# Exponentials folded in place behind the first product with v, one-step splits of q and k, a new planned order, and 23 early weight quarters

## The chip, the cores and the metric

The kernel runs on one core of one Trainium2 chip. The metric is the device time of one execution in microseconds; the time of a kernel is the median of its runs. A difference of less than about 0.5% can't be told from none here: the three runs shown below already lie within 0.4% of each other.

## The reference

Causal attention with a forget gate for 8 batches of 8 heads (576 positions, head size 64), and then a soft mixture of 8 experts over all 8 x 576 = 4608 tokens of width 512. All arrays are float32.

```python
scores = scale * np.matmul(q, k.transpose(0, 1, 3, 2))           # scale = 1/8
cum = np.cumsum(np.maximum(s, 0.0), axis=-1)
bias = -(cum[:, :, :, None] - cum[:, :, None, :])
scores = np.where(causal, -1000000000.0, scores + np.minimum(bias, 0.0))
scores = scores - np.max(scores, axis=-1, keepdims=True)
attn = np.exp(scores)
attn = attn / (np.sum(attn, axis=-1, keepdims=True) + 1e-09)
attn_out = np.matmul(attn, v)
...
x = attn_out.transpose(0, 2, 1, 3).reshape(B * S, H * D)
logits = x @ phi                                # 4608 x 32 slots
d = softmax(logits, over tokens);  slot_input = d.T @ x
h = relu(slot_input[e] @ w1[e]);  slot_out[e] = h @ w2[e]        # 4 slots for each expert
c = softmax(logits, over slots);  out = c @ slot_out
```

phi is 512 x 32, w1 is 8 x 512 x 1024, w2 is 8 x 1024 x 512: 33.6 MB of weights.

## The kernel before

**The work.** The heads are taken two at a time: 32 pairs, four for each batch, head 0 of a pair on partitions 0 to 63 and head 1 on 64 to 127. The scores proper are held with the keys on the partitions and the queries along the row, in five key blocks of 128, 128, 128, 128 and 64; what is zero by causality is left out but for the diagonal, so that one head's exponentials are rows of 576 + 448 + 320 + 192 + 64 = 1600. For a pair p the steps are:

- `load` (L268): q and k arrive by one DMA, 128 x 1152. `cast` (L278, ACT) rounds them to the reduced float type in which PE multiplies, `low` (L283, DVE) subtracts to get the remainder; both in two steps of 576, q and then k. `cum` (L293) brings the gate's sums into the tile g by DMA, `md` (L359) the row maxima.
- `mx` (L311, PE): a first set of scores, of the rounded parts alone and with the queries on the partitions, in groups `mx.0` to `mx.3`, for the row maxima; `red` (L323, DVE) takes the maxima. `f0` (L338 and L339, POOL) splits them in two parts, `f1` (L346, PE) transposes them, `f2` (ACT) copies, `md` sends them into g.
- `s` (L377, PE): the scores proper, three products of the parts and one with g, in four groups `s.0` to `s.3`. `ex` (L388, ACT) writes the exponentials into the pair's p buffer, `cut` (L395, POOL) zeroes what lies above the diagonal.
- The fold: the five key blocks are added up to one row of 576 in a z buffer of its own. `zc` (ACT) copies the first 128 columns, and `z.0` to `z.3` (L421, L423, L425, L427, POOL; DVE for the last pair) add the blocks.
- `ax` and `a` (L467 and L478, PE) are the first product with v in the text's words: the exponentials times v. ACT copies it out (`evx`, `ev`) into a u buffer.
- `sm` (L507, PE), the closing sum: 16 small products of z with `onesl`, a table of 16 blocks of ones, add up over the partitions. The four pairs of a batch collect in one bank. After a batch's last pair DVE takes reciprocals, a DMA writes them out (`rs<-sr`) and one for each pair reads them back spread over partitions (`rd`, L517, `arena<-rs`); `nr` (L540, DVE) multiplies. In the last batch pairs 28 and 29, pair 30, and pair 31 close apart.
- For each batch then: transposes (`nat`, L548), logits (`lt`, L619 and L623), softmax over slots (`s0` to `s2`; its last product, `s2p`, is L682 on POOL, `e_nat`), and the softmax over tokens as a running sum (`t2` to `t8`: L733, L756, L771), which gives slot inputs.

After the 32 pairs: slot inputs (`sit`, L941), the two products with the experts' weights (`mlp1`, L954; `mlp2`, L988), and the outputs (`po`, L1020; L1028), 18 transfers of 0.524 MB.

**The order.** Every step is declared with `op(key, engine, planned ns, due time, function, what it waits for, banks)`. Due times are two for each pair plus a number from the table `PR`. `schedule()` (L34) lists the steps in order by planned starts, with six PSUM banks for scores, maxima and transposes; the engines get exactly that order, so on each engine nothing overtakes. Where the plan shows PE idle before the first product with v, and after the last one, 128x128 dummy products (`busy`, L914) are inserted, one for each 300 ns.

**Buffers.** `NBUF` counts them in one tile, the arena: two p, one z, and so on. A p buffer is free for the pair after next when the product with v and the fold have read it.

**The weights.** They come in 64 quarters of 0.524 MB. The first `NPRE` = 21 go to a place of their own (`pre`) one for each pair from pair 4 on, without waiting for anything but a load of q and k; the others follow (`get`, L836), on the same SP queue, into g, w and arena chunks as these come free near the end, and then into the places of used weights (`refill`).

The initial memory fills stand ahead of everything else on DVE and POOL, with the sum of the gates on DVE.

Of the kernel before, what the change touches and what calls it, by code (L numbers as in the profile page):

```python
# [20 lines left out]
PR = dict(load=-9.063, load_v=-9.132, cast=(9.576, 4.001), cum=-25.895, low=(4.9, 44.265), mx=(-6.08, 10.156, 8.807,  # L21
          8.159), red=(2.144, 3.397, 3.057, -37.226), f0=-0.714, f1=30.964, f2=0.529, md=-6.393, s=(-65.95, -10.099,
          -16.585, -0.002), ex=(6.942, -14.568, 1.896, 3.855), cut=(1.377, -17.534, 2.864, 12.095), zc=3.583,
          z=(1.07, -54.955, 7.483, 3.74), ax=102.687, a=(136.656, 0.022, -2.121, 0.386, -0.338), evx=-22.47,
          ev=-3.276, sm=14.037, e1=-1.61, rw=24.679, rd=-39.652, nstep=4.53, nr=1.749, nat=48.432, natd=-28.53,
          lt=-51.395, nat0=116.745, natd0=17.779, c0=4.561, c1=-16.819, soft=15.188, tok=30.263, LA=161.4, ct=1.864,
          T2=-19.79, LP=176.8, gap=0.81401)
# [75 lines left out]
def tile_attn_softmoe(ctx: ExitStack, tc, qk, v, s, phi, w1, w2, cst, out):  # L103
# [74 lines left out]
    nc.vector.tensor_scalar(s_sb, s_sb, 0.0, 8.0, op0=ALU.max, op1=ALU.mult)  # L178
    nc.vector.tensor_tensor_scan(out=cum, data0=ones_s, data1=s_sb, initial=0.0,
                                 op0=ALU.mult, op1=ALU.add)  # L180
    cumhl = reg("x", 0)[0:NH, 0:2 * S].rearrange("p (l x) -> p l x", l=2)
    nc.vector.tensor_copy(cumhl[:, 0, :].bitcast(F32R), cum)
    nc.vector.tensor_tensor(cumhl[:, 1, :].bitcast(F32R), cum, cumhl[:, 0, :], op=ALU.subtract)
    cumd = pd.tile([NH, 2, S], F32, tag="cum", name="cumd", bufs=1)
# [10 lines left out]
    nc.gpsimd.memset(reg("x", 0)[64:128, 0:DM], 0.0)  # L195
    for i in range(NV):
        nc.gpsimd.memset(reg("v", i)[64:128, 512:640], 0.0)
    for i in range(NPB):
        nc.gpsimd.memset(reg("p", i).rearrange("p (a x) -> p a x", a=2)[64:128, :, 1536:1600], 0.0)
    ph = one.tile([128, HP, 4 * NS], F32, name="ph")  # L200

    QO, KO = PAD, PAD + S
    gs = []
    for i in range(NG):
        t = slot("g", [128, PAD + 2 * S], F32R, f"g{i}")
        if i == 1:

            mask = one.tile([128, S], F32, name="mask")  # L210
            nc.gpsimd.memset(mask, 0.0)
            nc.gpsimd.affine_select(mask[:, S - 128:S], mask[:, S - 128:S], pattern=[[-1, 128]], compare_op=ALU.is_ge,
                                    fill=NEG, base=0, channel_multiplier=1)
        (nc.vector if i else nc.gpsimd).memset(t.bitcast(F32), 0.0)
        for a in (0, 64):
            nc.gpsimd.memset(t[a:a + 4, 0:KO].bitcast(F32), 1.0)
            nc.gpsimd.memset(t[a:a + 4, KO:].bitcast(F32), -1.0)  # L217
        gs.append(t)
    ws = []
    for i in range(NW):  # L220
        t = slot("w", [128, PAD + 4 * S], F32R, f"w{i}")
        nc.gpsimd.memset(t[:, 0:PAD].bitcast(F32), 0.0)
        ws.append(t)
# [30 lines left out]
    def scores(p):  # L254

        t0 = 2.0 * p
        gt, w = gs[p % NG], ws[p % NW]
# [17 lines left out]
        def cast(i):
            use("raw", p, NR)
            own("w", p, NW)
            nc.scalar.copy(w[:, QO + S * i:QO + S * (i + 1)], st["raw", p][:, i, :])  # L278

        def low(i):  # L280
            use("raw", p, NR)
            use("w", p, NW)
            nc.vector.tensor_tensor(w[:, QO + S * (2 + i):QO + S * (3 + i)], st["raw", p][:, i, :],  # L283
                                    w[:, QO + S * i:QO + S * (i + 1)].bitcast(F32), op=ALU.subtract)
# [828 lines left out]
```

## Time and profile before

| | |
|---|---|
| time, median of three runs (all of them) | 446.05 us (446.85, 446.05, 444.98) |
| profiled execution, and its span | 441.82 us, 440.1 us |
| mean granted PE clock | 0.978 of full speed |
| busy: PE, DVE, POOL, ACT | 406.3, 309.6, 281.4, 245.4 us (92%, 70%, 64%, 56%) |
| main DMA queue | 82.29 MB, 59.6% of 16 engines' time |
| HBM read, written | 71.84 MB, 10.06 MB |

The profile is of one execution, 1% faster than the median of the others. PE is the tensor engine, DVE the vector engine, ACT the scalar engine, POOL a second, general vector engine, and SP the engine that issues the DMAs; PE's weight loads overlap its products. In rows, "out<-in" are the program's names of the tiles, L478 is a line of the kernel, x20 a count of instructions. A row of the chain of work that ended last begins with start and duration in us. A timeline's row begins in the same way; what stands in brackets at its end is the idle time just before the row and what ended it. A row of a windows view has, after the window, its length, then busy time of PE, PE's weight loads, DVE, ACT and POOL (with the counts of instructions), the granted clock, the DMA share, and GB/s. In the row of clocks each digit is a fortieth of the span, in tenths of full speed.

### The profile page before, as it was taken

How to read it: one execution, taken by the hardware profiler on the slowest of the kernel's cores; microseconds unless marked ns; L12 is line 12 of the kernel's file. 1: busy time of each engine (PE TensorE's matmuls, PEld its weight loads, DVE VectorE, ACT ScalarE, POOL GpSimd, SP SyncE). 2: the span in 40 equal slices, each digit the busy share in tenths (PEclk: the TensorE clock that was granted, in tenths of full speed). 3: DMA queues.
4: the chain of work that ended last, by engine and by line, in shares of the span. 5: the costliest groups of instructions: out<-in, count | busy, mean ns of one | idle time of the engine just before them, and what ended most of it. 6: DMA issues, size and time to landing. Idle time of an engine off the chain costs nothing.

```text
span 440.1 us, 14686 instructions
## 1 busy us (share of the span) xinstructions
PE 406.3 (92%) x5625; PEld 302.5 (69%) x5625; DVE 309.6 (70%) x1055; ACT 245.4 (56%) x732; POOL 281.4 (64%) x385
## 2 busy tenths in 40 slices
PE   7999999989999999999999999999999999898960
PEld 6787777777677767766877687777776857344550
DVE  6777767987887888779877887788778486121460
ACT  3146676576658665856675676567665745011350
POOL 7349889878877895888588858887887710000000
PEclk9599999999999999999999999999999999999995
DMA  5317565626664475448544822362247389999988
GB/s 175 108 57 236 157 174 155 212 87 189 193 180 131 137 217 157 131 136 225 152 132 136 231 90 84 105 178 82 87 114 216 95 291 337 392 402 409 384 297 293
DMA packets 54549, 83.21 MB, mean 189 GB/s; under 512 B 5456, under 2 KB 41808, under 8 KB 54480
## 3 DMA queue, kind: packets, MB, share of 16 engines
q1 hardware_dynamic: 54480, 82.29, 59.6%
q8 instruction: 44, 0.72, 0.7%
q14 instruction: 25, 0.20, 0.1%
HBM read 71.84 MB, written 10.06 MB: 186 GB/s over the span
## 4 chain that ended last, share of the span: by engine, by line
PE 66%; DMA 12%; DVE 9%; issue 5%; SPq 3%; POOL 2%; ACT 1%; DVEq 0%
PE s L377 19%; PE y L478 15%; PE mx L311 10%; DMA arena<-rs 7%; PE m L954 3%; DMA rs<-sr 3%; PE m L988 3%; PE sum L507 3%; SPq L517 2%; DVE nmin L733 2%; PE busy L914 2%; PE lt L619 2%; PE nat L548 2%; PE po L1020 2%; DVE junk L323 1%
## 5 line engine op out<-in xcount | busy, mean ns | idle before, releaser
L323 DVE CUSTOM_DVE_ANT_0 junk<-mx,mask 128x448 bf16<-128x448 f32 (+3 forms) x320 | 125.5, 427 | 50.8 <-PE mx L311 25.1
L388 ACT ACTIVATE arena<-s 128x288 f32<-128x288 f32 (+4 forms) x384 | 114.3, 409 | 30.0 <-PE s L377 29.3
L377 PE MATMUL s<-w 64*128 64x288 f32 (+4 forms) x1152 | 109.2, 304 | 0.0
L478 PE MATMUL y<-arena 128*64 128x512 f32 (+4 forms) x640 | 90.1, 427 | 0.0
L377 PEld LDWEIGHTS s<-w 64*128 64x128 f32 (+1 forms) x1152 | 81.7, 177 | 10.1 <-ACT arena L388 1.2
L395 POOL TENSOR_SCALAR_AFFINE_SELECT arena<-arena 128x256 f32<-128x256 f32 (+1 forms) x160 | 69.0, 444 | 23.7 <-ACT arena L388 21.7
L478 PEld LDWEIGHTS y<-arena 128*64 128x64 f32 x640 | 43.0, 137 | 46.4 <-issue 35.8
L421 POOL TENSOR_TENSOR arena<-arena 128x896 f32<-128x896 f32 x31 | 66.4, 2141 | 7.5 <-PE mt L346 5.2
L311 PE MATMUL mx<-w 64*128 64x288 f32 (+4 forms) x384 | 59.3, 314 | 3.7 <-DVE e_nat L664 2.7
L311 PE MATMUL mx<-g,ones 64*128 64x288 f32 (+4 forms) x384 | 56.0, 308 | 1.7 <-DVE ones L227 1.7
L377 PE MATMUL s<-g 64*128 64x288 f32 (+4 forms) x384 | 56.5, 291 | 0.0
L423 POOL TENSOR_TENSOR arena<-arena 128x640 f32<-128x640 f32 x31 | 48.0, 1547 | 2.6
L278 ACT CAST w<-arena 128x576 fp32r<-128x576 f32 x64 | 39.8, 675 | 15.0 <-DMA arena<-in_qk_dram 15.0
L283 DVE TENSOR_TENSOR w<-arena,w 128x576 fp32r<-128x576 f32 x64 | 48.0, 776 | 0.0
L311 PEld LDWEIGHTS mx<-w 64*128 64x128 f32 x384 | 41.1, 190 | 8.1 <-PE s L377 3.8
L490 ACT COPY arena<-y 128x512 f32<-128x512 f32 x32 | 18.8, 588 | 47.0 <-PE y L478 47.0
L311 PEld LDWEIGHTS mx<-g,ones 64*128 64x128 f32 x384 | 41.0, 191 | 2.4 <-POOL g L217 1.9
L540 DVE TENSOR_TENSOR arena<-arena 128x576 f32<-128x576 f32 x31 | 34.7, 1128 | 8.7 <-DMA arena<-rs 8.4
L377 PEld LDWEIGHTS s<-g 64*128 64x128 f32 (+1 forms) x384 | 35.1, 177 | 0.7 <-DMA g<-hl 0.2
L338 POOL TENSOR_SCALAR mh<-mx 128x10 fp32r<-128x10 f32 x32 | 21.5, 672 | 20.4 <-DVE mx L323 20.3
L425 POOL TENSOR_TENSOR arena<-arena 128x384 f32<-128x384 f32 x31 | 31.4, 1013 | 2.4
L323 DVE CUSTOM_DVE_ANT_0 junk<-mx,mask,mx 128x288 bf16<-128x288 f32 x64 | 30.6, 516 | 2.2 <-PE mx L311 1.2
(157 smaller groups left out, 565.8 us busy)
## 6 DMA issues: line engine op xcount, KB each, us to landing
pre<-in_w_dram SPq DMA_DIRECT2D x38, 512.0 KB
arena<-in_qk_dram SPq DMA_DIRECT2D x32, 576.0 KB
...
```

The costliest lines, as they stand in the source:

```text
L278: nc.scalar.copy(w[:, QO + S * i:QO + S * (i + 1)], st["raw", p][:, i, :])
L283: nc.vector.tensor_tensor(w[:, QO + S * (2 + i):QO + S * (3 + i)], st["raw", p][:, i, :], w[:, QO + S * i:QO + S * (i + 1)].bitcast(F32), ...
L311: nc.tensor.matmul(ps[a][:, d:d + hi - lo], l[r], t[r, KO + lo:KO + hi], start=t is w, stop=t is gt)
L323: nc.vector.tensor_tensor_reduce(out=junk[r, 0:w], in0=ps[r, d:d + w], in1=mask[r, o:o + w], scale=1.0, scalar=m[:, a, 4:5] if i == 1 else ...
L377: nc.tensor.matmul(ps[a][0:n, d:d + hi - lo], t[r, ko + 128 * j:ko + 128 * j + n], t[r, qo + lo:qo + hi], start=x == 0, stop=x == 3)
L388: nc.scalar.activation(st["p", p][0:n, a, o + lo:o + hi], ps[0:n, d:d + hi - lo], AF.Exp, bias=0.0, scale=0.125)
L395: nc.gpsimd.affine_select(d, d, pattern=[[0, 2], [1, n]], compare_op=ALU.is_ge, fill=0.0, base=0, channel_multiplier=-1)
L421: eng.tensor_tensor(z[:, :, 128:576], pt[:, :, 128:576], pt[:, :, 576:1024], op=ALU.add)
L423: eng.tensor_tensor(z[:, :, 256:576], z[:, :, 256:576], pt[:, :, 1024:1344], op=ALU.add)
L425: eng.tensor_tensor(z[:, :, 384:576], z[:, :, 384:576], pt[:, :, 1344:1536], op=ALU.add)
L478: nc.tensor.matmul(y[r, lo - 64:512], vt[:, j, r], st["p", p][:, g, OFF[j] + lo - 128 * j:OFF[j] + 576 - 128 * j], start=(j == 0), stop=(j ...
L540: nc.vector.tensor_tensor(u, u, st.pop(("r", p)), op=ALU.mult)
```

## The change

It edits the program at these places:

1. The z buffer and `zc` are gone. The fold adds the blocks into the p buffer itself, at the columns where block 0 stands. Since the product reads these columns as exponentials, `z.0` waits for `a.0`, the product's first part (L469 in the new text). The closing sum reads the p buffer, and the exponentials of the pair after next wait for the sum.
2. `cast` and `low` are one step each of 1152 columns. Planned 1045 and 1500 ns instead of twice 565 and 950.
3. `onesl` is one row of 63 with a single column of ones, of which a window of 32 is taken; `phi` is stored once and not four times; `junk` and `en` have one buffer each, so that a batch's `sp` waits for the `ct` of the batch before.
4. The initial fills: `ones2` and `mx` come first on DVE, the mask and the first g tile first on POOL; the other two g tiles are steps of their own (`gi`) on POOL. The due times of pair 0's steps up to the exponentials are lowered by 200 (`tu`).
5. `NPRE` is 23. Without the z buffer the arena has 16 chunks for weights, not 17; With the places in g and w there were 22 quarters fetched by `get`, now 21, and 20 `refill` quarters follow instead of 21.
6. The table `PR` has other numbers throughout, which gives another order on every engine.

```diff
-NBUF = (2, 2, 2, 1, 5, 2, 3)
+NBUF = (2, 2, 2, 5, 2, 3)
-NPRE = 21
+NPRE = 23
...
-        for i in range(2):
-            op(("cast", p, i), "ACT", 565, (t0, ("cast", i)), (cast, i), [("load", p)] + war)
-            op(("low", p, i), "DVE", 950, (t0, ("low", i)), (low, i), [("cast", p, i)])
+        op(("cast", p), "ACT", 1045, (tu, "cast"), cast, [("load", p)] + war)
+        op(("low", p), "DVE", 1500, (t0, "low"), low, [("cast", p)])
...
-        war = [("a", g, j) for j in range(5)] + [("ax", g), ("z", g, 3), ("zc", g)] if g is not None else []
+        war = [("a", g, j) for j in range(5)] + [("ax", g), ("sm", g)] if g is not None else []
...
-            st["z", p] = reg("z", p % NZ).rearrange("p (a x) -> p a x", a=2)
-            nc.scalar.copy(st["z", p][:, :, 0:128], st["p", p][:, :, 0:128])
...
-            if i == 0:
-                eng.tensor_tensor(z[:, :, 128:576], pt[:, :, 128:576], pt[:, :, 576:1024], op=ALU.add)
-            elif i == 1:
-                eng.tensor_tensor(z[:, :, 256:576], z[:, :, 256:576], pt[:, :, 1024:1344], op=ALU.add)
...
+            n = 64 if i == 3 else 128
+            d = pt[0:n, :, 128 * (i + 1):576]
+            eng.tensor_tensor(d, d, pt[0:n, :, OFF[i + 1]:OFF[i + 1] + 448 - 128 * i], op=ALU.add)
...
-               zd[i] + [("z", p, i - 1) if i else ("zc", p)])
+               zd[i] + [("z", p, i - 1) if i else ("a", p, 0)])
...
-                        nc.tensor.matmul(y[o:o + 32, 0:SQ], onesl[:, 4 * hp + i, :], st["z", p][:, g, c:c + SQ],
+                        nc.tensor.matmul(y[o:o + 32, 0:SQ], onesl[:, 31 - 4 * hp - i:63 - 4 * hp - i], st["p", p][:, g, c:c + SQ],
...
-    for e, ns in (("DVE", 5200), ("POOL", 4200), ("SP", 1100), ("ACT", 2900), ("PE", 1100)):
+    for e, ns in (("DVE", 7000), ("POOL", 6200), ("SP", 700), ("ACT", 2900), ("PE", 1100)):
         op(("set", e), e, ns, (-1000,), lambda: None)
+    for i in range(1, NG):
+        op(("gi", i), "POOL", 2400, (2.0 * i - 10,), (ginit, i), [("set", "POOL")])
```

In the rows below, taken from the order of the instructions on an engine, there is no time; the number behind a tile's name is the pair or the batch with the group, and the last one counts tiles.

**The start, on SP's queue**, before: s is the gate, qk one pair's q and k, g the tile of gate sums and row maxima.

```order
L176 DMA arena_77<-in_s_dram 64x576
L447 DMA arena_77<-in_v_dram 128x4x128
L450 DMA arena_77<-in_v_dram 64x128
L268 DMA arena_77<-in_qk_dram 128x1152
L447 DMA arena_77<-in_v_dram 128x4x128
L450 DMA arena_77<-in_v_dram 64x128
L268 DMA arena_77<-in_qk_dram 128x1152
L293 DMA g0_128<-arena_77 2x1x576 x2
L293 DMA g1_134<-arena_77 2x1x576 x2
L293 DMA g2_145<-arena_77 2x1x576 x2
L268 DMA arena_77<-in_qk_dram 128x1152
L853 DMA cumd_101<-arena_77 64x1152
```

and now (L272 is the load of q and k, L296 the gate sums):

```order
L176 DMA arena_77<-in_s_dram 64x576
L272 DMA arena_77<-in_qk_dram 128x1152 x2
L438 DMA arena_77<-in_v_dram 128x4x128
L441 DMA arena_77<-in_v_dram 64x128
L438 DMA arena_77<-in_v_dram 128x4x128
L441 DMA arena_77<-in_v_dram 64x128
L296 DMA g0_123<-arena_77 2x1x576 x2
L296 DMA g1_124<-arena_77 2x1x576 x2
L272 DMA arena_77<-in_qk_dram 128x1152
L296 DMA g2_125<-arena_77 2x1x576 x2
L272 DMA arena_77<-in_qk_dram 128x1152
L846 DMA cumd_116<-arena_77 64x1152
```

The first two pairs' q and k stand ahead of all of v. On PE, 31 dummies stand ahead of the first maxima instead of 25, and all four groups of maxima of pair 0 ahead of the first of pair 1, where the group `mx.1` of pair 0 used to stand behind a group of pair 1; ahead of the first scores stand a transpose and four dummies, where eleven stood.

**A batch's third pair, on POOL**, batch 3 with pair 14, before (a fold is the rows L421, L423, L425, L427):

```order
L395 AFFINE_SELECT arena_77<-arena_77 128x2x128 x3
L395 AFFINE_SELECT arena_77<-arena_77 64x2x64
L421 TENSOR_TENSOR arena_77<-arena_77 128x2x448
L682 TENSOR_TENSOR e_nat_66<-e_nat_66,cs2_3373 128x160
L395 AFFINE_SELECT arena_77<-arena_77 128x2x128
L423 TENSOR_TENSOR arena_77<-arena_77 128x2x320
L425 TENSOR_TENSOR arena_77<-arena_77 128x2x192
L427 TENSOR_TENSOR arena_77<-arena_77 64x2x64
L338 TENSOR_SCALAR mh16_3481<-mx1_163 128x2x5
L339 TENSOR_TENSOR mh16_3481<-mx1_163,mh16_3481 128x2x5
```

and now (L398 cuts, L420 is the whole fold, L341 and L342 split the row maxima, L673 is the last product of the softmax over slots):

```order
L398 AFFINE_SELECT arena_77<-arena_77 128x2x128 x3
L398 AFFINE_SELECT arena_77<-arena_77 64x2x64
L398 AFFINE_SELECT arena_77<-arena_77 128x2x128
L341 TENSOR_SCALAR mh16_3364<-mx1_108 128x2x5
L342 TENSOR_TENSOR mh16_3364<-mx1_108,mh16_3364 128x2x5
L673 TENSOR_TENSOR e_nat_66<-e_nat_66,cs2_3417 128x160
L420 TENSOR_TENSOR arena_77<-arena_77 128x2x448
L420 TENSOR_TENSOR arena_77<-arena_77 128x2x320
L420 TENSOR_TENSOR arena_77<-arena_77 128x2x192
L420 TENSOR_TENSOR arena_77<-arena_77 64x2x64
```

The cuts stand ahead of the fold as a block, and the softmax's product, which stood behind the fold's first addition, stands ahead of it, as do the two steps on the maxima of pair 16.

**A plain pair, on PE**, the closing sum of pair 16 before:

```order
L311 MATMUL mx0_19_1_3918<-g1_134,ones2_157 128x288
L507 MATMUL sum16_3924<-arena_77,onesl_102 32x72 x16
L346 MATMUL mt_3950<-ident_61,mh18_3876 20x128
L548 MATMUL nat12_3952<-ident_61,arena_77 128x128 x4
L377 MATMUL s17_3_0_3964<-w2_155 128x320
```

and now:

```order
L314 MATMUL mx3_19_1_3875<-g1_124,ones2_102 128x192
L349 MATMUL mt_3891<-ident_61,mh18_3833 20x128
L498 MATMUL sum16_3897<-arena_77,onesl_97 32x72 x16
L314 MATMUL mx2_19_0_3927<-w1_132 128x448
L314 MATMUL mx2_19_1_3928<-w1_132 128x448
```

Before, the first product of pair 16 with v begins 32 rows behind this sum. Now it began 67 rows ahead of it, and the row of L469 that begins pair 17's stands 13 rows behind.

**The end, on PE**, before (L709 and L756 are transposes of the two softmaxes' rows, x and y the first product):

```order
L377 MATMUL s31_3_1_6890<-g1_134 128x320
L507 MATMUL sum30_6902<-arena_77,onesl_102 32x72 x16
L709 MATMUL ctb0_6926<-ident_61,en0_1861 96x128
L709 MATMUL cta0_6925<-ident_61,en0_1861 96x128 x4
L756 MATMUL dn6_6939<-ident_61,dt6_6811 128x128
L757 MATMUL dn6_6939<-ident_61,dt6_6811 64x128
L467 MATMUL x31_6943<-arena_77 64x64 x2
L478 MATMUL y30_6951<-arena_77 64x512 x2
```

and now:

```order
L380 MATMUL s31_3_1_6785<-g1_124 128x320
L498 MATMUL sum30_6802<-arena_77,onesl_97 32x72 x16
L700 MATMUL ctb0_6826<-ident_61,en0_1761 96x128
L700 MATMUL cta0_6825<-ident_61,en0_1761 96x128 x4
L747 MATMUL dn6_6839<-ident_61,dt6_6704 128x128
L748 MATMUL dn6_6839<-ident_61,dt6_6704 64x128
L469 MATMUL y31_6847<-arena_77 64x512 x2
```

Sum 30 used to stand ahead of product 30; now that product stands 53 rows ahead of it, with all of pair 31's scores between, and product 31 follows behind.

More of the change, by code (lines that the diff above doesn't have):

```diff
@@ L19 @@
 NG = 3
[L21 to L27, printed above, removed]
-NBUF = (2, 2, 2, 1, 5, 2, 3)
+PR = dict(load=-7.139, load_v=-2.32, cast=3.046, cum=-6.431, low=83.254, mx=(-43.805, 4.895, 4.715, 3.882),
+          red=(30.0, 18.855, 7.742, 5.31), f0=0.185, f1=23.061, f2=3.709, md=-16.796, s=(-21.112, -1.186, -26.288,
+          2.204), ex=(8.386, -2.546, 24.758, 5.631), cut=(13.379, 1.043, 13.216, -8.496), z=(5.742, 0.566, 8.913,
+          -16.511), ax=6.788, a=(2.526, -8.101, -13.574, -16.298, 7.51), evx=0.756, ev=-10.922, sm=14.574,
+          e1=-15.72, rw=-1.196, rd=-3.926, nstep=7.841, nr=0.118, nat=-32.994, natd=-18.393, lt=6.769, nat0=-3.935,
+          natd0=1.004, c0=-30.944, c1=-6.683, soft=25.805, tok=86.831, LA=142.6, ct=45.552, T2=45.669, LP=237.6,
+          gap=2.995)
+NBUF = (2, 2, 2, 5, 2, 3)
 NBANK = 6
 GAP = 300
-NPRE = 21
+NPRE = 23
 def schedule(ops, banks):
@@ L177, in tile_attn_softmoe @@
     nc.vector.memset(ones_s, 1.0)
[L178 to L184, printed above, removed]
     SQ = S // 8
-    onesl = one.tile([128, 4 * HP, 32], F32, name="onesl")
+    onesl = one.tile([128, 63], F32, name="onesl")
     nc.vector.memset(onesl, 0.0)
-    for a in range(4 * HP):
-        nc.vector.memset(onesl[:, a, a:a + 1], 1.0)
+    nc.vector.memset(onesl[:, 31:32], 1.0)
     dn = one.tile([128, 2, 128], F32, name="dn")
     nc.vector.memset(dn[64:128, 1, :], 0.0)
[L195 to L223, printed above, removed]
     ones2 = one.tile([128, 128], F32R, name="ones2")
@@ L232, in tile_attn_softmoe, with ginit @@
         mx.append(t)
+    nc.vector.tensor_scalar(s_sb, s_sb, 0.0, 8.0, op0=ALU.max, op1=ALU.mult)
+    nc.vector.tensor_tensor_scan(out=cum, data0=ones_s, data1=s_sb, initial=0.0,
+                                 op0=ALU.mult, op1=ALU.add)
+    cumhl = reg("x", 0)[0:NH, 0:2 * S].rearrange("p (l x) -> p l x", l=2)
+    nc.vector.tensor_copy(cumhl[:, 0, :].bitcast(F32R), cum)
+    nc.vector.tensor_tensor(cumhl[:, 1, :].bitcast(F32R), cum, cumhl[:, 0, :], op=ALU.subtract)
+    cumd = pd.tile([NH, 2, S], F32, tag="cum", name="cumd", bufs=1)
+    ph = one.tile([128, HP, NS], F32, name="ph")
+    mask = one.tile([128, S], F32, name="mask")
+    nc.gpsimd.memset(mask, 0.0)
+    nc.gpsimd.affine_select(mask[:, S - 128:S], mask[:, S - 128:S], pattern=[[-1, 128]], compare_op=ALU.is_ge,
+                            fill=NEG, base=0, channel_multiplier=1)
+    QO, KO = PAD, PAD + S
+    gs = [slot("g", [128, PAD + 2 * S], F32R, f"g{i}") for i in range(NG)]
+    def ginit(i):
+        t = gs[i]
+        nc.gpsimd.memset(t[:, 0:KO].bitcast(F32), 1.0)
+        nc.gpsimd.memset(t[:, KO:].bitcast(F32), 0.0)
+        for a in (0, 64):
+            nc.gpsimd.memset(t[a:a + 4, KO:].bitcast(F32), -1.0)
+    ginit(0)
+    ws = []
+    for i in range(NW):
+        t = slot("w", [128, PAD + 4 * S], F32R, f"w{i}")
+        nc.gpsimd.memset(t[:, 0:PAD].bitcast(F32), 0.0)
+        ws.append(t)
+    nc.gpsimd.memset(reg("x", 0)[64:128, 0:DM], 0.0)
+    for i in range(NV):
+        nc.gpsimd.memset(reg("v", i)[64:128, 512:640], 0.0)
+    for i in range(NPB):
+        nc.gpsimd.memset(reg("p", i).rearrange("p (a x) -> p a x", a=2)[64:128, :, 1536:1600], 0.0)
     OFF = [0, 576, 1024, 1344, 1536]
@@ L340, in f0 @@
             st["mh", p] = mh
-        op(("f0", p), "POOL", 850, (t0, "f0"), f0, [("red", p, i, a) for i in range(4) for a in range(2)] + [dep("f1", old(2))])
+        op(("f0", p), "POOL", 850, (tu, "f0"), f0, [("red", p, i, a) for i in range(4) for a in range(2)] + [dep("f1", old(2))])
         def f1():
@@ L347, in f1 @@
             st["mt", p] = ps
[L348 removed]
+        op(("f1", p), "PE", 110, (tu, "f1"), f1, [("f0", p), dep("md", old(2))], bank=1, ldw=17)
         def f2():
@@ L353, in f2 @@
             st["hl", p] = hl
-        op(("f2", p), "ACT", 160, (t0, "f2"), f2, [("f1", p)], frees=[(("f1", p), 0)])
+        op(("f2", p), "ACT", 160, (tu, "f2"), f2, [("f1", p)], frees=[(("f1", p), 0)])
         def md():
```

69 lines of the change are left out of this document (30 added, 39 removed).

## The prediction

> Times are microseconds. "Pair p" is a pair of heads, Y(p) the start of its first product with v on PE, and "fold" the four POOL additions that add up a pair's exponentials.
>
> **What bounds the kernel now.** I read the page's first rows, then the chain that ended last in order of time, then POOL's and DVE's instructions at the places that the change moves, then the tail by windows.
>
> ```profile
> span 440.1 us, 14686 instructions
> PE 406.3 (92%) x5625; PEld 302.5 (69%) x5625; DVE 309.6 (70%) x1055; ACT 245.4 (56%) x732; POOL 281.4 (64%) x385
> ...
> PEclk9599999999999999999999999999999999999995
> ...
> 43.96 2.81 PE s L377 x40
> ...
> 47.03 0.64 PE sum L507 x32
> ...
> 47.88 0.79 PE s L377 x8
> 48.67 1.41 PE mx L311 x20
> 50.08 2.74 PE y L478 x20
> 52.82 0.12 PE x L467 x4
> ```
>
> Up to about 375 PE sets the pace: a plain pair is these pieces and, where a line is left out, 0.26 of maxima and 0.21 of a transpose, without a gap: 8.96 from 43.96 to 52.94. POOL is nearly as full inside a pair:
>
> ```profile
> 184.43 2.12 POOL L421 TENSOR_TENSOR arena<-arena 128x896 f32<-128x896 f32 x1
> 186.50 0.41 POOL L395 TENSOR_SCALAR_AFFINE_SELECT arena<-arena 128x256 f32<-128x256 f32 x1
> ...
> 190.10 0.75 POOL L338 TENSOR_SCALAR mh<-mx 128x10 fp32r<-128x10 f32 x1
> 190.94 0.54 POOL L339 TENSOR_TENSOR mh<-mx,mh 128x10 fp32r<-128x10 f32 x1
> ```
>
> From the first row to the end of the last lie a fold's four additions and the two steps on the row maxima: 7.05, or 6.6 without the cut (L395 and its gap, 0.49) that stands among them; the two steps are 1.4 of it. The pair's other cuts, four of 0.41 or less, fill most of what is left of 8.96. The tail has other limits:
>
> ```profile
> 352.45 0.68 PE sum L507 x32
> ...
> 354.05 6.96 DMA rs<-sr
> ...
> 361.70 4.36 DMA arena<-rs
> ...
> 366.08 0.77 DVE arena L540
> ...
> 373.14 0.99 PE sl L771 x8
> ...
> 376.91 1.05 PE sit L941 x8
> ...
> 407.84 4.72 DMA out_dram<-arena
> ...
> 420.00:430.00 10.00, 5.50 (x40) 4.62 (x38) 6.21 (x11) 5.59 (x12) 0.00 (x0) 1.00 0.85 291
> 370.00:407.84 37.84, 34.18 (x373) 17.36 (x370) 10.34 (x30) 8.09 (x22) 0.46 (x1) 1.00 1.02 403
> ```
>
> Pair 30's closing sum ends at 353.13; its reciprocals go out (6.96) and back (4.36) past weights, and the normalised rows are there at 366.85. From 376.91 to the first output at 407.84 PE works on, waiting for no weight. Then 18 outputs of 0.524 MB leave: 9.44 MB in 32.3 is 292 GB/s, and from 420 to 430, when no weight moves any more, the rate is the same (the last figure of a window's row, 291). So the end is the first output plus 32.3.
>
> **The start: -4.1.** These rows give what stands before the first scores:
>
> ```profile
> 1.41 7.37 PE L914 MATMUL busy<-ident 128*128 128x128 f32 x50 [1.41 <-POOL ident masks.py:199]
> 7.69 1.25 ACT L278 CAST w<-arena 128x576 fp32r<-128x576 f32 x2 [5.62 <-DMA arena<-in_qk_dram]
> 11.12 0.75 PE L311 MATMUL mx<-g,ones 64*128 64x288 f32 x2 [1.74 <-DVE ones L227]
> 11.35 0.74 DVE L283 TENSOR_TENSOR w<-arena,w 128x576 fp32r<-128x576 f32 x1
> 12.68 0.45 DVE L323 CUSTOM_DVE_ANT_0 junk<-mx,mask 128x288 bf16<-128x288 f32 x1
> 19.13 0.25 POOL L338 TENSOR_SCALAR mh<-mx 128x10 fp32r<-128x10 f32 x1 [4.60 <-DVE mx L323]
> 22.40 0.27 PE L346 MATMUL mt<-ident,mh 128*20 128x128 f32 x1
> 22.99 1.32 SPq L359 DMA_DIRECT2D g<-hl  x2
> 23.95 2.72 PE L914 MATMUL busy<-ident 128*128 128x128 f32 x22
> 26.60 0.67 PE L377 MATMUL s<-w 64*128 64x288 f32 x6
> ```
>
> q and k of pair 0 are asked for about 1.2 earlier, ahead of v. One cast of 1152 costs about the 1.25 of two (saving 0.1, taken as nothing). The ones that PE waited for until 11.12 are now written first on DVE. Against that, 31 opening dummies replace 25: six more at 2.72/11 = 0.25 put PE's first product at 10.3. DVE has both pairs' splits ahead of the maxima (four of 0.74 by this profile's row, an estimated 2.8 as two), the second waiting for pair 1's cast at about 9.6; so the maxima start at 11.0, not 12.68. Their own instructions for one pair fill 5.0 of the 6.45 between 12.68 and 19.13; PE's order now has all of pair 0 ahead of pair 1, so I take 5.0 twice: pair 0 at 16.0, pair 1 at 21.0, the latter's transpose at 22.3. Pair 0's own rows, behind the third cast on ACT, land by 17.8 + 3.7 = 21.5 (22.99 to 26.67 is 3.7 at most), so they are covered. Scores start at 22.3 instead of 26.60: -4.3, of which waits for banks give 0.2 back. Bounds: both pairs of maxima at the old pace (6.45) leave -1.4; landings 1.4 earlier than I took give -5.5. I take -4.1, since its terms are this profile's own instructions.
>
> **The pair: a new loop.** Before, a pair's fold ran beside the scores ahead of its first product, and its closing sum stood ahead of that product on PE. The fold now works in place and so waits for the first part of the product; the sum stands behind product and scores and waits for the fold. From Y(p): that part is 512 of 1536 columns of 2.74, 0.9, and with the hand-over 1.1 (0.2 is an estimate between nothing and the 0.32 from the end of PE's transpose at 22.67 to the issue at 22.99, which has a copy on ACT in it); fold and maxima 6.6; hand-over 0.1: the sum can start at 7.8. PE gets there after products 2.86, maxima 0.26, scores 3.39, maxima 0.48 and a transpose of 0.15: 7.15. It waits 0.65, then sum 0.64 and maxima 0.95: 9.45 instead of 8.96. Pairs 2 and 3 differ (9.0 and 9.6). Y(0) to Y(5) comes to 46.9 against 31.00 to 76.99: **+0.9**. The removed copy gives nothing: ACT, 56% busy, is nowhere in this loop. The p buffer now frees at the closing sum, a whole product ahead of the scores that overwrite it: nothing.
>
> **The batches: -3.0 once, then -0.5.**
>
> ```profile
> 31.00 1.78 PE L478 MATMUL y<-arena 128*64 128x512 f32 x8
> 76.99 2.81 PE L478 MATMUL y<-arena 128*64 128x512 f32 x20
> 100.04 2.81 PE L478 MATMUL y<-arena 128*64 128x512 f32 x20
> 315.04 2.81 PE L478 MATMUL y<-arena 128*64 128x512 f32 x20
> ...
> 342.39 0.36 PE lt L619 x8
> ...
> 343.73 0.11 PE lt L623 x8
> ...
> 344.77 0.87 PE nat L548 x8
> ```
>
> The first batch's close takes 23.05 between Y(5) and Y(6), and 27.0 with product 6 (2.64) and the token sums (0.99 and 0.3), which the new order does before Y(7). The new order's pieces from Y(5) to Y(6): product 2.64, scores of one pair 3.39 and half of the next 1.9, maxima 2.0, sum 0.64, logits 1.45 (the eight lt rows from 342.39), nine groups of transposes of 0.44 or 0.2, 3.0: 15.0, and 0.35 for copies that free banks. The normalised rows that they take are 17 to 20 behind the batch's last sum, and before they were used 14 to 20 behind it; so I add no wait. From Y(6) to Y(7): 1.1, the fold alone 5.2, 0.1, sum 0.64, token sums 1.2: 8.25. With 0.4 for small gaps 24.0, where before PE had some 4 of waiting for rows: **-3.0**. Afterwards a batch takes 43.0 (100.04 to 315.04 is five); the new one two looped pairs, 18.9, + 15.35 + 8.25 + 0.4 = 42.9: **-0.5** over five. A batch has an uncertainty of 0.8, so this term reaches from -4.5 to +3.5.
>
> **The end: +4.2, +0.8 and +0.4.** Before, sum 30 preceded product 30; now it follows it, its folds and all scores of pair 31. From Y(27) the new order needs 9.5 + 9.5, 12.1 to Y(30) (two transposes wait 1 for rows), 6.55 to the folds' end and 0.65 for the sum: 38.3, where before took 34.1 from the equal point (Y(26) + 4.0) to 353.13: **+4.2**. The trip of the reciprocals queues behind four quarters and not three on its way back (+1.3) but 0.85 further from the two ahead of it (-0.5): **+0.8**. Two transposes (0.87) stand ahead of the last logits, half covered: **+0.4**.
>
> **Two quarters early: nothing.** Each is 0.524 MB, 1.3 at the 403 GB/s that flowed from 370 to 408, so 2.6 if weights set the end. But PE waits for none, and outputs leave at 292 GB/s with and without weights beside them. Bounds 0 and -2.6; I take 0. The two transfers that move in among the pairs cost nothing unless a row transfer stands behind one: 1.3 at most.
>
> Sum: -4.1 + 0.9 - 3.0 - 0.5 + 4.2 + 0.8 + 0.4 = **-1.3**. The profiled execution took 441.82, 1.7 around its span; the runs shown have a median of 446.05, 1% higher. I put the change on the median: **444.7**.
>
> **Rivals.**
> (a) The front's gain survives: the end costs 1.5, not 5.4, because the sum of pair 30 is early enough, and the batches run at the bare 42.5. For it: ACT has 0.41 less per pair, and DVE fewer instructions. Against it: the order of sum 30. -1.3 - 3.9 = -5.2, 440.9.
> (b) Slower: on POOL the softmax's product now stands ahead of all four folds of a batch's third pair, not among them. Before it made POOL wait:
>
> ```profile
> 176.55 0.46 POOL L682 TENSOR_TENSOR e_nat<-e_nat,cs 128x160 f32<-128x160 f32 x1 [1.91 <-ACT arena L388]
> ```
>
> By my walk it is done 0.5 before the first fold could start. From there each microsecond of lateness is one for the fold, the sum and PE, in seven batches; 1.3 beyond the margin is +9: 453.7. For it: ACT has a long row of copies ahead of its exponential; against: no fold runs beside DVE's softmax steps any more.
> (c) A cold start. The page's clock row has 5 in its second slice, where PE sat idle around 9 to 11; the new order has one to four dummies where it waits for maxima, instead of eleven ahead of the scores. If the scores start at that clock, 3.39 becomes about 6: +2.6, 447.3. The Trainium skill (TensorE: Matmul & The Clock Gate, What's actually happening) says that an idle window of about 3.4 halves the clock and as much work restores it. By that rule the waits here, 1 to 3, would seldom do it, and the sum would stay; the row agrees so far as its 5 stands at the longest idle stretch of the start.
> (d) The early quarters do pay, -2.6: 442.1.
>
> **Chances.** The forecast's own case 0.36 (range 442.2 to 447.5), (a) 0.27, (b) 0.17, (c) 0.10, (d) 0.10. A measurement tells 0.5%, 2.2, from no change. Faster holds (a), most of (d) and a quarter of the forecast's case: 0.44; slower holds (b), a third of (c) and the upper edge of the forecast's: 0.25; the rest, 0.31, is no change. The range reaches to (a) less another 2.9 for its uncertain batches, and into (b): 438.0 to 451.5.
>
> **What would show it.** First scores at 22 to 23; plain pairs of 9.4 to 9.5 with PE idle ahead of the closing sum until a fold ends; Y(6) near 89; batches of 43; pair 30's sum ending near 350 to 352; first output at 405 to 408 and 32.3 from there to the end. Wrong if plain pairs stay at 9.0, if POOL waits for the softmax ahead of a fold, or if the outputs take less than 31.

## The result, and the profile after

The changed kernel takes 477.49 (475.06 to 479.06), the one before, beside it, 445.51: a ratio of 1.076, interval 1.071 to 1.081, slower by 32. The forecast was 444.7. The profiled execution has a span of 476.3, 36.2 more than before. From the page of the changed kernel:

```profile
span 476.3 us, 14797 instructions
PE 433.8 (91%) x5639; PEld 323.9 (68%) x5639; DVE 318.7 (67%) x1006; ACT 234.8 (49%) x668; POOL 276.7 (58%) x384
...
PEclk9999999899999998999799999998999999899996
...
PE 63%; DVE 19%; issue 6%; POOL 5%; DMA 4%; ACT 1%; DVEq 0%; SPq 0%; POOLq 0%
```

The last of these rows on the page before:

```profile
PE 66%; DMA 12%; DVE 9%; issue 5%; SPq 3%; POOL 2%; ACT 1%; DVEq 0%
```

On the chain that ended last DVE has gone from 9% to 19%, though its busy time grew by 9, to 318.7 of 476. So DVE is not full, but waited for. The windows of plain pairs, of three batch closes and of the pair behind one (window, length, busy times, clock) show where:

```profile
109.92:119.49 9.57, 9.20 (x132) 7.12 (x130) 6.85 (x21) 5.67 (x16) 8.39 (x12) 1.00 0.51 179
119.49:129.07 9.58, 9.58 (x131) 7.31 (x129) 7.52 (x30) 5.57 (x17) 8.19 (x12) 1.00 0.56 155
129.07:147.65 18.58, 16.72 (x250) 13.25 (x248) 16.39 (x50) 10.15 (x30) 10.75 (x15) 1.00 0.57 172
147.65:156.12 8.47, 8.40 (x117) 5.82 (x115) 4.49 (x17) 5.25 (x17) 7.13 (x10) 1.00 0.22 54
...
175.18:194.70 19.52, 17.88 (x250) 14.51 (x248) 16.47 (x51) 10.20 (x30) 10.29 (x15) 0.91 0.54 163
...
222.33:243.68 21.35, 19.50 (x250) 16.13 (x248) 16.49 (x51) 10.46 (x30) 10.80 (x15) 0.84 0.48 149
```

Plain pairs (9.6) and the pair behind a close (8.5) are near the forecast (9.45 and 8.25 to 8.65). A close was to take 15.35; it takes 18.6 to 21.4, with DVE busy for 16.4 of it. Three things are behind that. First, DVE's maxima, shown at the start of the program, where they follow each other with hardly a wait; the kernel before, then the changed one:

```profile
13.05 0.45 DVE L323 CUSTOM_DVE_ANT_0 junk<-mx,mask 128x288 bf16<-128x288 f32 x1
...
13.43 0.48 DVE L323 CUSTOM_DVE_ANT_0 junk<-mx,mask 128x320 bf16<-128x320 f32 x1
```

```profile
11.54 0.46 DVE L326 CUSTOM_DVE_ANT_0 junk<-mx,mask 128x288 bf16<-128x288 f32 x1 [1.55 <-PE mx L314]
...
12.15 0.46 DVE L326 CUSTOM_DVE_ANT_0 junk<-mx,mask 128x288 bf16<-128x288 f32 x1
...
18.31 0.46 DVE L326 CUSTOM_DVE_ANT_0 junk<-mx,mask 128x288 bf16<-128x288 f32 x1
```

The durations are the same, but the second begins 0.61 behind the first and not 0.37 (before, the first began at 12.68), and a pair's twelve take 6.77 (11.54 to 18.31). Their output, `junk`, which nobody reads, has one buffer now. Second, a close on DVE, POOL and PE:

```profile
128.83 0.78 DVE L531 TENSOR_TENSOR arena<-arena 128x576 f32<-128x576 f32 x1
...
130.46 2.56 DVE L531 TENSOR_TENSOR arena<-arena 128x576 f32<-128x576 f32 x1
133.05 0.62 DVE L326 CUSTOM_DVE_ANT_0 junk<-mx,mask 128x448 bf16<-128x448 f32 x1
...
130.31 4.10 POOL L420 TENSOR_TENSOR arena<-arena 128x896 f32<-128x896 f32 x2 [0.44 <-PE y L469]
...
134.10 0.85 PE L380 MATMUL s<-w 64*128 64x448 f32 x5 [1.55 <-DVE mx L326]
```

The same normalisation takes 0.78 alone and 2.56 when it begins 0.15 behind the fold's first addition (2.1): 1.95 of waiting for that to end, and 0.61. It stands ahead of the maxima (133.05) that hold the bank in which PE's next scores go. Third, the granted clock (the third figure from the end of a row) behind that wait of PE, in this close and in another:

```profile
129.45:132.86 3.41, 3.10 (x25) 1.57 (x21) 3.35 (x6) 0.00 (x0) 2.90 (x3) 1.00 0.71 201
132.86:136.28 3.42, 1.99 (x23) 1.73 (x24) 2.75 (x12) 0.98 (x2) 2.36 (x4) 1.00 0.63 150
136.28:139.69 3.41, 3.38 (x47) 3.11 (x45) 3.38 (x7) 3.08 (x12) 3.33 (x5) 1.00 0.58 186
...
225.02:228.43 3.41, 1.84 (x19) 1.22 (x13) 3.05 (x8) 0.07 (x1) 2.58 (x2) 1.00 0.54 151
228.43:231.84 3.41, 3.23 (x32) 3.23 (x34) 3.09 (x8) 2.06 (x6) 3.03 (x5) 0.50 0.66 215
231.84:235.26 3.42, 3.42 (x25) 3.25 (x24) 1.50 (x6) 1.94 (x7) 1.74 (x5) 0.50 0.55 181
235.26:238.67 3.41, 3.41 (x89) 2.94 (x91) 2.23 (x9) 2.62 (x4) 0.35 (x1) 1.00 0.38 95
```

It falls to 0.50 for 6.8, and this close is 2.8 longer than the one at 129.07, whose wait is the same 1.55 and whose clock stays at 1.00. The windows are cut where the clock can change: in each trace here all its changes lie whole multiples of 3.41 apart. The wait that ends at 227.36 lies whole in one such stretch, in which PE is busy for 1.84; the one that ends at 134.10 is cut at 132.86, and PE is busy for 1.99 in the poorer half. Over all sixteen traces, from Y(0) to Y(27), a stretch at 1.00 is followed by a fall in all 7 cases in which PE was busy for less than half of it, in 13 of the 16 with 50 to 55%, and in 2 of the 1341 fuller ones.

### The profile page after: what moved, and what is told of

It reads as the page before. It is cut to its first block, busy times and chain, and to the rows that moved or that the text cites. A ratio compares the mean times of both kernels' runs of the same rounds, so it can differ in the third digit from the quotient of the medians.

```text
span 476.3 us, 14797 instructions
## 1 busy us (share of the span) xinstructions
PE 433.8 (91%) x5639; PEld 323.9 (68%) x5639; DVE 318.7 (67%) x1006; ACT 234.8 (49%) x668; POOL 276.7 (58%) x384
## 4 chain that ended last, share of the span: by engine, by line
PE 63%; DVE 19%; issue 6%; POOL 5%; DMA 4%; ACT 1%; DVEq 0%; SPq 0%; POOLq 0%
PE s L380 18%; DVE junk L326 11%; PE y L469 11%; PE mx L314 9%; POOL arena L420 5%; DVE arena L531 4%; PE m L947 3%; PE m L981 3%; PE busy L907 3%; PE sum L498 3%; PE nat L539 3%; DMA arena<-rs 2%; DVE w L287 2%; PE po L1013 2%; PE lt L610 2%
## 5 line engine op out<-in xcount | busy, mean ns | idle before, releaser
L420 POOL TENSOR_TENSOR arena<-arena 128x896 f32<-128x896 f32 (+1 forms) x124 | 183.9, 1483 | 39.1 <-PE y L469 33.7
L326 DVE CUSTOM_DVE_ANT_0 junk<-mx,mask 128x448 bf16<-128x448 f32 (+2 forms) x320 | 137.6, 430 | 79.1 <-PE mx L314 56.7
L380 PEld LDWEIGHTS s<-w 64*128 64x128 f32 (+1 forms) x1152 | 98.6, 189 | 27.8 <-issue 12.6
L469 PE MATMUL y<-arena 128*64 128x512 f32 (+4 forms) x640 | 92.0, 427 | 0.4 <-ACT arena L481 0.4
L469 PEld LDWEIGHTS y<-arena 128*64 128x64 f32 x640 | 41.6, 137 | 47.2 <-issue 34.4
L380 PE MATMUL s<-g 64*128 64x288 f32 (+4 forms) x384 | 72.6, 304 | 0.0
L398 POOL TENSOR_SCALAR_AFFINE_SELECT arena<-arena 128x256 f32<-128x256 f32 (+1 forms) x160 | 61.9, 418 | 8.6 <-ACT arena L391 8.6
L380 PEld LDWEIGHTS s<-g 64*128 64x128 f32 (+1 forms) x384 | 51.3, 190 | 0.2
L287 DVE TENSOR_TENSOR w<-arena,w 128x1152 fp32r<-128x1152 f32 x32 | 48.0, 1499 | 0.4 <-ACT w L282 0.4
L282 ACT CAST w<-arena 128x1152 fp32r<-128x1152 f32 x32 | 36.7, 1148 | 13.8 <-DMA arena<-in_qk_dram 13.8
L341 POOL TENSOR_SCALAR mh<-mx 128x10 fp32r<-128x10 f32 x32 | 8.3, 259 | 49.4 <-DVE mx L326 49.4
L326 DVE DVE_READ_ACCUMULATOR2_ANT mx<- 128x1 f32 (+1 forms) x384 | 31.6, 82 | 0.0
L498 PE MATMUL sum<-arena,onesl 128*32 128x72 f32 x1024 | 25.6, 230 | 0.3
```

Source lines behind the costliest of these rows:

```text
L282: nc.scalar.copy(w[:, QO:QO + 2 * S], st["raw", p].rearrange("p i s -> p (i s)"))
L287: nc.vector.tensor_tensor(w[:, QO + 2 * S:QO + 4 * S], st["raw", p].rearrange("p i s -> p (i s)"), w[:, QO:QO + 2 * S].bitcast(F32), op=AL ...
L326: nc.vector.tensor_tensor_reduce(out=junk[r, 0:w], in0=ps[r, d:d + w], in1=mask[r, o:o + w], scale=1.0, scalar=m[:, a, 4:5] if i == 1 else ...
L380: nc.tensor.matmul(ps[a][0:n, d:d + hi - lo], t[r, ko + 128 * j:ko + 128 * j + n], t[r, qo + lo:qo + hi], start=x == 0, stop=x == 3)
L398: nc.gpsimd.affine_select(d, d, pattern=[[0, 2], [1, n]], compare_op=ALU.is_ge, fill=0.0, base=0, channel_multiplier=-1)
L420: eng.tensor_tensor(d, d, pt[0:n, :, OFF[i + 1]:OFF[i + 1] + 448 - 128 * i], op=ALU.add)
```

## The experiments

Each median stands beside a median of the kernel before from the same or earlier runs, 442.4 to 444.2.

**Two junk buffers.** e1 is the changed kernel with

```diff
-                junk = p2.tile([128, 448], BF16, tag="junk", name="junk", bufs=1)
+                junk = p2.tile([128, 448], BF16, tag="junk", name="junk", bufs=2)
```

and e2 the kernel before with the opposite edit (`bufs=1` put in). The order on all engines stays the same in both.

> The changed kernel with two junk buffers, as before, in place of one; the order on every engine is the same. Theory A (the single junk buffer makes every maximum on DVE wait for the end of the one before it: twelve of a pair take 6.7 instead of 5.0, in all 32 x 1.75 = 56 of DVE time, and through the six banks PE waits for DVE): the 31 us that were lost come back, 438 to 449, maxima of pair 0 in 5.0, batch closes of 15 to 16 instead of 18.6 to 21.4. Rival B (the new order bunches a batch's normalisations and softmax in one close, and a normalisation on DVE beside a fold on POOL takes 2.6 instead of 0.8): DVE is full in the closes anyway, 465 or more. Rival C (PE's idle stretches drop the granted clock in the closes): that follows the waits, and goes with them under A; by itself it is 1 to 1.5 a batch, so 465 to 470 would be left.

> The kernel before with one junk buffer instead of two, nothing else, the order the same. Theory A: DVE is only 70% busy, but its maxima free the banks that PE's next scores need; 56 of DVE time more make this 15 to 35 slower than before, 460 to 481. Rival B: DVE's 130 of idle time take most of it, at most 5 slower.

Measured: e1 464.35 (ratio 1.047, interval 1.041 to 1.053), e2 455.86 (1.026, 1.020 to 1.032). The buffer is worth 12 to 13 in either kernel: put into the one it costs 12, taken out of the other it gives back 13. But that is less than half of the loss: for e1 theory A was right in kind and wrong in size, for e2 the cost lies between the two theories, and the closes of e1 still take 17.8 to 19.3. Of e1's maxima, twelve take 4.88:

```profile
11.66 0.46 DVE L326 CUSTOM_DVE_ANT_0 junk<-mx,mask 128x288 bf16<-128x288 f32 x1 [0.77 <-PE mx L314]
12.04 0.45 DVE L326 CUSTOM_DVE_ANT_0 junk<-mx,mask 128x288 bf16<-128x288 f32 x1
...
16.54 0.46 DVE L326 CUSTOM_DVE_ANT_0 junk<-mx,mask 128x288 bf16<-128x288 f32 x1
```

**The other halved buffer.** e3 takes `bufs=1` from `en`.

> The changed kernel with the other buffer that it halves, en (a batch's split softmax rows), doubled again; one junk buffer stays. Theory A: no change against the changed kernel, 475 to 479, since the copies into en come once a batch and wait for transposes long done. Rival B would have part of the closes' wait here: 3 to 8 faster.

475.77, 1.7 less than the changed kernel and within the spread of either (4.0 and 2.2): no change, as theory A had it. Its closes are those of the changed kernel to 0.02 from the second on (18.57, 19.53, 21.33).

**The early quarters.** e4 is e1 with steps 21 and 22 of the early fetches emptied, so that their quarters come last:

```diff
-        op(("pre", i), ..., (get, pre[:, 1024 * i:1024 * (i + 1)]), ...)
+        op(("pre", i), ..., (get, pre[:, 1024 * i:1024 * (i + 1)]) if i < 21 else lambda: None, ...)
```

> As the first of these runs (two junk buffers), but the two additional early weight quarters are not fetched early: they are fetched last, as refills, and there are 22 refills. The prediction's step (early quarters are worth nothing, since PE waits for no weight and the outputs leave at their own rate): within 1 of the first run. Rival D (weights set the end): 2.6 slower than the first run.

464.74 against 464.35. Each has a spread of 5 to 6, so the times alone don't rule out rival D's 2.6. The traces speak against it: PE waits for no weight in either, and from the issue of the first output to the end both take 33.9. No cost is seen, as forecast.

**No fold.** e5 is e1 without POOL's additions (`if p == NP - 1:` ahead of them), so its sums are of other rows.

> The changed kernel with two junk buffers (464.4), and the fold on POOL left out for pairs 0 to 30 (the closing sums then add up the wrong rows), the order otherwise the same. Theory A (a subtraction or a normalisation on DVE runs at less than half its pace while POOL adds: low 2.05 instead of 1.35, normalisations 1.34 in the mean instead of 0.77, up to 2.55 in the batch closes, where PE waits for the maxima behind them): low 1.35 to 1.4, all normalisations 0.75 to 0.8, the wait of 1.55 ahead of the scores in the closes gone, plain pairs 9.0, closes 15.5 to 16: 440 to 448. Rival B (PE's order alone sets it): DVE's instructions shorter, but plain pairs stay at 9.4 and closes over 17: over 458.

436.98, 27 less than e1, a little under theory A's range; its plain pairs take 9.0 to 9.1 and its closes 15.8 to 16.2, as theory A had it but for 0.2. The 27 hold all that the fold costs: what it does to DVE, and the closing sum's wait for it. On DVE (mean ns of one behind the busy time), e1 first, then e5:

```profile
L287 DVE TENSOR_TENSOR w<-arena,w 128x1152 fp32r<-128x1152 f32 x32 | 65.5, 2048 | 1.3 <-ACT w L282 1.3
L531 DVE TENSOR_TENSOR arena<-arena 128x576 f32<-128x576 f32 x31 | 41.4, 1337 | 5.8 <-DMA arena<-rs 5.5
```

```profile
L287 DVE TENSOR_TENSOR w<-arena,w 128x1152 fp32r<-128x1152 f32 x32 | 43.3, 1353 | 0.0
...
L532 DVE TENSOR_TENSOR arena<-arena 128x576 f32<-128x576 f32 x31 | 24.4, 790 | 9.8 <-DMA arena<-rs 9.4
```

In the kernel before, with its fold, the normalisations have 1128. So what stretches both is the fold beside them.

**The normalisation behind the maxima.** e6 is e4 with a third buffer for broadcast rows, and

```diff
+    for b in range(B - 1):
+        behind(("nr", HP * b + 1), ("red", HP * b + 8, 0, 1) if b < B - 2 else ("red", NP - 1, 1, 1))
```

where `behind` moves a step in the finished order. (In the last of these closes this puts the step behind its transposes too, which then take rows that aren't normalised.)

> Two junk buffers, 21 early quarters, and in seven closes the second normalisation on DVE stands behind the maxima whose banks PE's scores need, not between them (a third buffer for the broadcast rows makes that possible). Theory A: PE's wait of 1.55 at the scores of each close (1.9 with the first one's start) goes, closes of about 16, and no dip of the granted clock there: 7 x 1.9 = 13 and some 4 for the clock, 447 to 453. Rival B: the normalisation holds up what now stands behind it (the next remainder, the transposes), and the wait comes back later in the close: 460 to 464.

447.06, 17.7 less than e4: the wait goes, and the dips of the clock with it. Of the 21.8 between the two spans (462.9 and 441.1), 4.5 is a start that came early by the landing of a load, told below (Y(0) at 27.27 and not 31.75). Its close, with the plain pair ahead:

```profile
108.53:118.03 9.50, 9.43 (x131) 7.24 (x129) 8.31 (x30) 5.47 (x16) 8.30 (x12) 1.00 0.53 156
118.03:133.87 15.84, 15.84 (x250) 13.19 (x248) 13.93 (x49) 9.75 (x30) 11.10 (x15) 1.00 0.67 199
```

**Pair 2's load.** e7 is e1 with two steps of SP moved: load 2 behind the gate rows of pair 1, load 3 behind those of pair 2.

> Two junk buffers, and at the start the load of pair 2's q and k goes out ahead of pair 2's gate rows and of pair 3's load (it stood behind both, and the gate rows wait for POOL's fill of the third g tile until 11.6). Theory A (PE's first scores come late because pair 2's first maxima stand ahead of pair 1's last on PE and wait for that load, which lands at 18.5): first scores at 22.5 to 23.5 instead of 26.5, whole 460 to 462. Rival B: the load lands as late, held up by the other transfers: no change, 464.

460.33, 4 less. The cast that PE's queue waits for (e1 first, then e7), and the first scores in the same order:

```profile
18.52 1.15 ACT L282 CAST w<-arena 128x1152 fp32r<-128x1152 f32 x1 [9.03 <-DMA arena<-in_qk_dram]
...
26.47 1.25 PE L380 MATMUL s<-w 64*128 64x448 f32 x6
```

```profile
13.40 1.15 ACT L282 CAST w<-arena 128x1152 fp32r<-128x1152 f32 x1 [4.96 <-DMA arena<-in_qk_dram]
...
22.11 0.87 PE L380 MATMUL s<-w 64*128 64x448 f32 x6
```

In e6 and in e8 the cast began at 17.3 to 17.4 with the load where it was, and the scores at 22.6 to 22.7. In e1 and e4 it began at 18.52 and 18.92, and the scores at 26.47 and 27.23. So the late start hangs on a landing that varies by 1.7, and a late one costs 4. Only 1.1 of e1's 3.7 against e6 is the later cast. The other 2.6 go with the clock, which falls behind PE's longer wait for the cast in e1 and stays at 1.00 in e6 (e1 first, then e6):

```profile
17.05:20.47 3.42, 1.76 (x17) 1.32 (x16) 3.33 (x18) 1.31 (x2) 0.21 (x1) 1.00 0.39 139
20.47:23.88 3.41, 3.41 (x18) 2.68 (x19) 1.48 (x9) 0.00 (x0) 0.31 (x2) 0.50 0.01 3
23.88:27.29 3.41, 3.41 (x19) 2.77 (x17) 3.01 (x11) 0.25 (x1) 0.13 (x1) 0.50 0.00 0
```

```profile
15.98:19.39 3.41, 2.31 (x19) 1.76 (x20) 3.35 (x19) 1.31 (x2) 0.46 (x2) 1.00 0.42 149
19.39:22.81 3.42, 3.42 (x31) 2.69 (x29) 2.84 (x15) 0.00 (x0) 0.45 (x2) 1.00 0.02 5
```

**The fold out of place.** e8 is e4 with a z buffer, ACT's copy into it ahead of the first addition, and the fold and the sum on it; the order stays, the wait for the product is gone.

> Two junk buffers, 21 early quarters, and the fold goes into a z buffer of its own again (with ACT's copy of the first 128 columns), so that it doesn't wait for the product's first part; it stands where it stood on every queue. The prediction's step (plain pairs pay 0.5 because fold and closing sum now wait for the product): folds start about 1 earlier, plain pairs 9.0, closes as they are: 448 to 455. Rival B (the fold's wait costs nothing; what holds plain pairs at 9.4 is DVE's remainder beside the fold): plain pairs 9.3 to 9.4, 461 to 466.

456.49 (453.46 to 461.83), 8.3 less than e4; its four times lie far apart, and of the 11.2 between the two profiled spans 4.7 is the landing just told, so the effect is read from the pairs. Pairs and a close:

```profile
98.97:107.98 9.01, 9.01 (x132) 7.07 (x130) 5.95 (x21) 5.87 (x18) 8.77 (x13) 1.00 0.61 208
107.98:116.99 9.01, 9.01 (x131) 7.04 (x129) 7.78 (x30) 5.80 (x19) 8.52 (x12) 1.00 0.57 158
116.99:134.93 17.94, 16.22 (x249) 13.22 (x247) 16.41 (x49) 10.09 (x32) 9.10 (x14) 1.00 0.59 179
```

The pairs are back at 9.0, the closes are not: the normalisation still stands where it stood.

**The mends together.** e9 is e6 with the load of e7, and with the seventh close left as it was. e10 adds on DVE: the remainder of pair p behind the first maxima of pair p (`behind(("low", p), ("red", p, 0, 1))`, with the loads that wait for it). e11 adds e8's z buffer to e10.

> Two junk buffers, 21 early quarters, the second normalisation behind the maxima in six closes (the last stays as it was), and pair 2's load ahead: three mends of waits on DVE and SP, in an order that is otherwise that of the change. Theory A (these three are what the forecast missed, and they add up: 477.5 - 12 for the buffers - 4 for the load - 15 for the normalisations and the clock): 445 to 449, first scores at 22 to 23, closes of 15.8. Rival B (a fixed wait uncovers another): over 452.

> As the run before (e9), and on DVE the remainder (1.35 alone, 1.9 to 2.05 beside the fold) stands behind the next pair's first maxima, not ahead of them. Theory A (plain pairs take 9.4 to 9.5 because PE's scores wait for the banks of those maxima): plain pairs 9.0 to 9.1, some 24 x 0.4 less: 436 to 441. Rival B (plain pairs take 9.4 because the closing sum waits for the fold, as the prediction had it): plain pairs stay at 9.4, within 1.5 of e9.

> As e10, and the fold goes into its own z buffer again, without the wait for the product. Theory A (folding in place costs only by where the fold falls beside DVE's work): within 2 of e10. Rival B (the closing sum waits for the fold): 5 to 9 faster than e10.

e9: 445.51 (1.008, 1.005 to 1.011): the three terms add up, and against e7, which has the other two mends, the normalisations with their clock are worth 14.8. e10: 450.37, e11: 454.16; both leave something out, since in pairs 30 and 31 the moved remainder comes behind weights that land in its place (DVE waits 4.3 and 4.4 for them) and reads those. So only their pairs up to 26 are read: plain pairs of 9.49 in e10 and 9.0 in e11. Rival B was right: the remainder's place does not matter, the fold's wait does. e9's chain of waits over one plain pair:

```profile
108.04 1.03 PE y L470 x4
...
109.21 2.10 POOL arena L421
...
111.38 1.57 POOL arena L421
112.95 1.33 POOL mh L342
...
114.56 0.97 POOL arena L421
...
115.61 0.46 POOL arena L421
...
116.11 0.33 PE sum L499 x6
```

That is the prediction's loop piece by piece: the product's first part, the four additions with the two steps on the maxima between them, and then the closing sum, which PE had reached at 115.3.

**One step instead of two, alone.** e12 is the kernel before with cast and remainder of 1152 put where their first halves stood.

> The kernel before, with cast and remainder in one step each, put where their first halves stood; nothing else. The prediction's step (one cast of 1152 costs what two of 576 cost, saving 0.1): no change, 441 to 445. Rival B (a remainder in one piece holds up the maxima that stood between its halves): 2 to 5 slower.

442.98 (1.0005, 0.997 to 1.004): no change.

**What is left, and whether the terms add.** e13 is e9 with the z buffer of e8, and both early normalisations of a close behind the maxima. e14 is e9 with one junk buffer.

> As e9 (two junk buffers, pair 2's load ahead, normalisation behind the maxima in six closes), with the fold in its own z buffer again; since that fold begins earlier, the first normalisation of a close stands behind the maxima too (four buffers for the broadcast rows, 20 early quarters for the room). Theory A (what is left of the change's cost is the fold's wait for the product): plain pairs 9.0 and 8.1 instead of 9.4, 9.5 and 8.5, closes of 15.8, so 1.25 a batch, 434 to 440, faster than the kernel before. Rival B (with the fold earlier, POOL and DVE collide elsewhere): batches of 43.2 as in e9, 443 to 448.

> As e9, with one junk buffer instead of two: of the three mends all but that one. Theory A (the terms add): e9 plus 12, 456 to 460. Rival B (the single junk buffer costs only where the normalisation stood in the maxima's way): under 450. Rival C (with the other waits gone DVE alone sets the pace): over 464.

e14: 460.76, 15 more than e9, so the single buffer costs 12 to 15 wherever it is put in. Of the 15, 4.0 are at the start (Y(0) at 30.66, in e9 at 26.66); between the profiles of the changed kernel and e1 they don't show, since e1's start was late by its landing (31.35). e13: 442.30, ratio 0.996, interval 0.993 to 0.998, the fastest here of those that leave nothing out, though the 0.4% to the kernel before is less than can be told from none. Its pairs are 9.0 and 8.1, its closes 16.5: a batch is 42.6 instead of 43.3, 0.7 less and not 1.25, because the fold then meets DVE elsewhere in the close: PE waits 0.55 for the first normalisation at 123.53 (both theories in part).

## Why the prediction was wrong

Spans: forecast 438.8, measured 476.3, a miss of 37.5. By the prediction's own terms, from Y(p) of the changed kernel and, in the last column, of e9:

| term | forecast | measured | in e9 |
|---|---|---|---|
| start, Y(0) against 31.00 | -4.1 | -0.4 | -4.3 |
| Y(0) to Y(5) against 45.99 | +0.9 | +5.0 | +1.6 |
| Y(5) to Y(7) | 24.0 | 28.4 | 24.3 |
| Y(7) to Y(27), five batches | 214.5 | 235.8 | 216.7 |
| Y(27) to the end | 126.5 | 130.6 | 128.8 |

- **The steps that failed** are two, both costs on DVE's queue, and the start's order adds a third, smaller one. The first is not in the sum at all: the change's part 3 gives `junk` one buffer, and the prediction puts no price on it. Twelve maxima were put at 5.0 at the start ("I take 5.0 twice"); they take 6.77 and 6.71, which in the changed kernel is the start's miss. Most of what is lost from Y(0) to Y(5) is of the same kind: from Y(2) to Y(3) it takes 12.45, with a fall of the clock, and e1 9.94. Over the whole kernel it is 12 to 15 of the 32.
- **The batches: "so I add no wait".** The rows that the normalisations need were counted; what stands behind a normalisation on DVE was not, nor what it meets on POOL. The fold's own start was worked out to 0.1 in the same text, and a normalisation with 0.78 alone and 1.13 in the mean stood in the profile before. This is 2.0 in each close by waiting (17.8 in e1, 15.8 in e9), and 0 to 2.8 more by the clock; 14.8 from e7 to e9. The Trainium skill (SBUF — State Buffer, Who interferes with whom) says that a DVE instruction with two inputs in SBUF contends with a GpSimd instruction that reads SBUF; by its section on the two separate sides the one that starts first holds the way for its whole length. The trace agrees: 2.56 is the rest of the addition, 1.95, and 0.61.
- **The start's order.** All of pair 0 does stand ahead of pair 1, but pair 2's first maxima stand ahead of pair 1's last, and its load went out behind the gate rows that wait for POOL's third fill. With that mended as well as the buffer (e7, e9) the start is the -4.1 of the forecast to 0.3. Either fault alone is enough to lose it: with the load ahead and one buffer (e14) Y(0) is 30.66, with two buffers and a late landing (e1) 31.35.
- **The pair was right**, in size (9.5 to 9.6 against 9.45, in the runs with two buffers 9.4 to 9.5; the terms given add up to 9.39) and in cause: without the wait it is 9.0 (e8, e11).
- **The end** was right in kind and too small: 4.1 more than the +5.4. Pair 30's sum ends 39.8 behind Y(27), where 38.3 was forecast; the reciprocals' trip takes 1.8 more than before, not 0.8 (its way back 6.6, not 4.36); and the first products with weights, at a mean clock of 0.88, take 11.93 instead of 10.51. From the issue of the first output to the end it is 33.9, in both kernels.
- **Early quarters at nothing, one-step splits at nothing**: right as far as e4 and e12 can tell.
- **The rivals.** (b) had the sign and not the place: in the trace the softmax's product is done at 147.7, 1.1 ahead of the fold at 148.82. (a) needed an end of +1.5; it was +9.5. (c) had the clock, but at the start; in the changed kernel the falls that count are in the closes and follow the waits there, while in e1 and e4, with the late landing, they are at the start too. The Trainium skill (TensorE: Matmul & The Clock Gate, What's actually happening) has the clock halve after an idle window of 3.4 that runs freely. The trace agrees on the grid of 3.41, but the window need not be idle: a wait of 1.55 was enough where it left PE busy for 1.84 of 3.41, and not where a boundary cut it. So waits shorter than the window can do it, which the prediction took to be seldom. What decides between 50 and 55%, where 3 of 16 did not fall, stays open.
- **The chances.** The 0.25 on slower rested on (b). No case had a cost on DVE's queue, though the profile before shows DVE 70% busy and its maxima as the costliest group.
